# Folding the tokens twice over d in a spectral gate plus dense layer, with accumulating transfers and a new order

## The chip, the cores and the metric

One core of a Trainium2 chip. The metric is the device time of one execution in microseconds: the median of three runs of the kernel before is 382.09 (381.73 to 382.65). Lower is better.

## The reference, cut to what matters

```python
g = sigmoid((x * gate_w).sum(-1))            # x: 2048 tokens (s) by 512 (d), float32
X = rfft2(x, axes=(s, d)) * (w_r + 1j*w_i)   # 2048 by 257 weights
a = irfft2(X)
h = gelu(x @ w1 + b1)                        # 512 -> 1792
b = h @ w2 + b2                              # 1792 -> 512
out = g * a + (1 - g) * b
```

## The kernel before, in words

**Numbers in two parts.** [...] So each operand is split into a high part (a rounding copy on ScalarE) and a low part (source minus high, on VectorE), and a product is three matmuls: high by high, high by low, low by high. All go through the helper at L400.

**The spectral half.** The 2048 tokens are 16 groups `j` of 128. `forward(j)` does, for each group in the order `NORD` (0, 4, 8, 12, 1, 5, ...): load `xf`; form the sum and the difference `eo` of the two halves of d (L552, two half-width VectorE instructions); split it into `eoh` and `eol` (L557, L559); multiply by the cosine and sine table `cf` into `pd`, of 258 columns (257 frequencies and the column with the gate's weights); split `pd` into `xh`, `xl` (L589, L590); sum the gate's logit (L592); transform over 128 tokens by the table `tf` into `py`; combine into the group's plane `y` (L609 to L619). Since `eo` folds d once, 256 rows remain: two chunks `q` of 128, each with its own table half. After that come steps over the 16 planes on VectorE (`stage1`, `filt` with the weights `wf`, `stage4`), a small correction (`own_rows`: `own`, `pown`, `yfix`), and `inverse(c, h)`, eight times: turned planes `sw` (ScalarE), `pq`, the split `vh`, `vl` (L443, L444), products `pz` with `tg`, the split `zh`, `zl`, products `pa` with `ci`, a copy `od` (L850), and sums and differences `u`, `v`, `w` (L860 to L870).

**The dense half.** `mlp(half, c)` takes 512 tokens `c` and half of the 1792 hidden units: per 128 units a product `ph` (12 matmuls of 512 columns), gelu, a split into `g..h`, `g..l`; then four `po` of 21 matmuls each. The first half's `po` plus bias goes to a DRAM buffer `bacc` (L960, L965); the second half adds it: for `c` = 3 and 0 on VectorE (L963) and back into `bacc`, for 1 and 2 in `last` (L971, L973, L978) on the way out. `inverse` for 3 and 0 comes last of its `c` and itself subtracts the dense part times (1 - g) and writes `out` (L865, L873).

**The order.** Every piece is a `Step` with an engine, a planned cost and a rank. `Graph.schedule` plays the steps through with those costs; where an engine is free, the ready step with the lowest rank starts. What comes out is fixed: each engine then works through its own list in order and waits, by semaphores, where a datum isn't there. Ranks are a few constants (0 for `forward`, 1 `FEED`, 5 `BULK`). Buffers come from tagged pools (`slots`): `xr` has three, shared by the loads of `forward`, the token loads `xm` of the dense half, and `sw`. Transfers are issued by SyncE (SP); the kernel before issues none from GpSimd (POOL).

Of the kernel before, what the change touches and what calls it, by code (L numbers as in the profile page):

```python
# [26 lines left out]
CW = 272  # L27


FORD = np.concatenate([np.arange(0, HD, 2), np.arange(1, HD, 2), [HD]])  # L30
# [23 lines left out]
def _tables():  # L54

    d = np.arange(P)[:, None] + 0.5
    f = np.arange(NE)[None, :]
    th = 2 * np.pi * f * d / D
    cf = np.stack([np.cos(th), -np.sin(th)])
    cf[0][:, HD:] = 0.0  # L60
    cf[1][:, 0] = 0.0
    cf[1][:, HD + 1:] = 0.0
    cf = cf[:, :, FORD]

    cf = np.stack(_split(cf[:, :, :ND])).transpose(1, 2, 0, 3)
    cf = np.concatenate([cf, np.zeros((2, P, 2, CW - ND), np.float32)], 3)

# [48 lines left out]
SPARE = 0.4  # L116

# [215 lines left out]

@with_exitstack
def tile_kernel(ctx: ExitStack, tc: tile.TileContext, xt, w1, w2, b1, b2, x0g, wf, wrev, out, consts):
# [12 lines left out]
    slots = {"xr": 3, "wra": 3, "wrb": 2, "t2k": 7, "e2": 4, "z": 4, "ttab": 3, "xhl": 2, "wa": 2 * FA, "wb": 2 * FA, "hid": 2 * FA,  # L348
             "so": 2, "ba": 2, "bb": 1, "pf": 2, "pm": 4, "ti": 1}

    whole = ("xr", "wra", "wrb", "e2", "z", "ttab", "xhl", "wa", "wb", "hid", "so", "ba", "ctab", "gb")
# [59 lines left out]
    gs = one("gs", [P, 2, 2], parts=2)  # L411

    cft = buf("ctab", [P, 2, 2, 2, CW], F32R, "cf", parts=12)
    cfp = {(0, 0): (0,), (1, 0): (1,), (0, 1): (2, 3, 4), (1, 1): (5, 6, 7)}

    def cf(c, q):
        return cft.ap()[:, c, q]

    def cf_of(*cq):
        return [(cft, p) for k in cq for p in cfp[k]] + [(cft, g) for g in range(8, 12)]  # L420
# [5 lines left out]
    logit = one("logit", [P, NJ], parts=NJ, pool=sa)  # L426
# [20 lines left out]
    def minus(h, l, view, n, src, rest, rank):  # L447

        a(lambda: act.activation(view(l), view(h).bitcast(F32), AF.Copy, scale=-1.0), n, rest[0], rest[1], rank)
        acc(lambda: view(l), src, 256, [], rest[1], rank)  # L450


    def load_x(j, tag):
        x = buf("xr", [P, NQ, P], F32, f"x{tag}{j}")
        dma(lambda: sp.dma_start(x.ap(), xt[j]), 256, [], [x], j / 100 if tag == "f" and j in NORD[:4] else FEED)
        return x
# [17 lines left out]
    for j in NORD[1:4]:  # L474
        XF[j] = load_x(j, "f")
    for c in range(2):
        dma(lambda c=c: raw(cf(c, 0), cf_d[c]), 272, [], [(cft, k) for k in (c, 8 + c, 10 + c)], 0.6)
# [8 lines left out]
    gcol = [lambda k=k: cft.ap()[:, :, :, k, NE - 1] for k in range(2)]  # L486
    tiny(lambda: vec.tensor_copy(gcol[0](), gs.ap()), [gs], [(cft, 8), (cft, 9)])
    tiny(lambda: vec.tensor_tensor(gcol[1](), gs.ap(), gcol[0](), op=ALU.subtract), [gs, (cft, 8), (cft, 9)], [(cft, 10), (cft, 11)])
    for c in range(2):

        def same(c=c):
            s = slice(0, P) if c == 0 else slice(P, HD)
            vec.tensor_copy(cf(c, 1)[:, :, s], cf(c, 0)[:, :, s])

        def other(c=c):
            s = slice(P, HD) if c == 0 else slice(0, P)
            act.mul(cf(c, 1)[:, :, s], cf(c, 0)[:, :, s], -1.0)

        def end(c=c):
            vec.tensor_scalar(cf(c, 1)[:, :, HD:ND], cf(c, 0)[:, :, HD:ND], -1.0, None, op0=ALU.mult)  # L500

        for e, f, n, k in ((v, same, 256, 0), (a, other, 256, 1), (v, end, 2, 2)):
            e(f, n, [(cft, c)], [(cft, 2 + 3 * c + k)], 0)

    def load_small():
        dma(lambda: sp.dma_start(b1t.ap(), b1), 7, [], [b1t], 0.45)
        dma(lambda: sp.dma_start(b2t.ap(), b2), 2, [], [b2t])
        dma(lambda: sp.dma_start(rev.ap(), wrev), 32, [], [rev])
# [15 lines left out]
    def keep_x(c):  # L524

        late = [Y[NORD[9]]] if c == 0 else []
        for k, b in zip("hl", X[0, c]):
            for j in range(4):
                dma(lambda k=k, b=b, j=j: sp.dma_start(xs[c, k].ap()[:, :, j], b.ap()[:, :, j].bitcast(F32)), 256,
                    [(b, j), *late], [(xs[c, k], j)], 6)  # L530

    def load_mx(half, c):
# [4 lines left out]
        if half == 0:  # L537
            for j1 in range(4):
                split_1(X[0, c], load_x(c + 4 * j1, "m"), j1)
# [6 lines left out]
    def forward(j):  # L546
        first = j == 0
        x = XF.pop(j) if j in XF else load_x(j, "f")
        eo = buf("t2k", [P, 2, 2, P], F32, f"eo{j}", parts=2)
        h, l = (buf("e2", [P, 2, 2, P], F32R, f"eo{k}{j}", parts=2) for k in "hl")  # L550
        for s, op in ((0, ALU.add), (1, ALU.subtract)):
            v(lambda s=s, op=op: vec.tensor_tensor(eo.ap()[:, s], x.ap()[:, 0:2], x.ap()[:, 2:4], op=op), 256, [x],  # L552
              [(eo, s)], FEED)
        for k in (0, 1) if first else (slice(0, 2),):
            ps = [k] if first else [0, 1]
            sub = [[(b, p) for p in ps] for b in (eo, h, l)]
            a(lambda k=k: act.activation(h.ap()[:, k], eo.ap()[:, k], AF.Copy), 256 * len(ps), sub[0], sub[1],  # L557
              FEED)
            v(lambda k=k: vec.tensor_tensor(l.ap()[:, k], eo.ap()[:, k], h.ap()[:, k], op=ALU.subtract),  # L559
              256 * len(ps), sub[0] + sub[1], sub[2], FEED)  # L560
        if j % 4 == 0:
            if first:
                X[0, 0] = new_x(0, 0)
# [3 lines left out]
        ps = buf("pf", [P, 2, 512], F32, f"pd{j}", parts=2, pool=pq)  # L567

        def high(qs=(0, 1), cs=(0, 1)):
            for q in qs:  # L570
                for c in cs:
                    mm(ps.ap()[:, c, :NE], h.ap()[:, c, q], cf(c, q)[:, 0, :NE], q == 0, False)
                    mm(ps.ap()[:, c, :NE], h.ap()[:, c, q], cf(c, q)[:, 1, :NE], False, False)

        def low():
            for c in range(2):
                for q in range(2):
                    mm(ps.ap()[:, c, :NE], l.ap()[:, c, q], cf(c, q)[:, 0, :NE], False, q == 1)

        if first:  # L580
            for q in range(2):
                for c in range(2):
                    m(lambda q=q, c=c: high((q,), (c,)), NE, 2, [(h, c), *cf_of((c, q))], [(ps, c)], 0)
        else:
            m(high, NE, 8, [h, cft], [ps], 0)
        m(low, NE, 4, [l, cft], [ps], 0)
        xh = buf("z", [P, 2, 512], F32R, f"x{j}h")
        xl = buf("z", [P, 2, 512], F32R, f"x{j}l")
        a(lambda: act.activation(xh.ap()[:, :, :NE], ps.ap()[:, :, :NE], AF.Copy), 516, [ps], [xh], 0)  # L589
        v(lambda: vec.tensor_tensor(xl.ap()[:, :, :NE], ps.ap()[:, :, :NE], xh.ap()[:, :, :NE], op=ALU.subtract), 516, [ps, xh], [xl], 0)  # L590
        n = j % 4 * 4 + j // 4
        v(lambda: vec.tensor_reduce(logit.ap()[:, n:n + 1], ps.ap()[:, :, NE - 1], axis=mybir.AxisListType.X, op=ALU.add),  # L592
          30, [ps, xl], [(logit, n)], 0)
# [11 lines left out]
        for c in range(2):  # L605
            m(lambda c=c: s_high(c), NE, 2, [t, xh], [py[c]], 0)
# [477 lines left out]
```

## Time and profile before

| what | value |
|---|---|
| median of three runs | 382.09 us |
| the profiled execution: from its first to its last instruction (span) | 380.0 us |
| what the median has beyond that span | 2.1 us |
| PE busy | 374.5 us (99%) |
| VectorE (DVE) busy | 338.4 us (89%) |
| ScalarE (ACT) busy | 207.8 us (55%) |
| DMA, mean | 149 GB/s |

The page gives no other time of the profiled execution than its span, so all sums below are made against 380.0 us and 2.1 us are added at the end. PE's busy time is drawn with modelled ends; where PE's pace matters, the distance from one start to the next is the number to use. Lines "SPq" are transfers being issued.

### The profile page before, as it was taken

The numbers are of one execution on the slowest core, as the hardware profiler recorded it, in microseconds if no ns is written. First come the engines' busy times: TensorE is split into PE (matmuls) and PEld (weight loads), VectorE is DVE, ScalarE is ACT, GpSimd is POOL, SyncE is SP. The second block draws the span as 40 slices with busy tenths as digits, with TensorE's granted clock in tenths as the row PEclk, the third lists the DMA queues.
The fourth block names the chain that finished last, engine by engine and source line by source line (L and its number), as shares of the span: only waits on it lengthen the run. The fifth ranks groups of instructions, "written<-read, shape, count | busy, mean of one in ns | idle before, by whom it ended". The sixth has DMA issues, their size and how long they took to land.

```text
span 380.0 us, 5499 instructions
## 1 busy us (share of the span) xinstructions
PE 374.5 (99%) x1903; PEld 319.1 (84%) x1903; DVE 338.4 (89%) x705; ACT 207.8 (55%) x363; POOL 0.2 (0%) x4
## 2 busy tenths in 40 slices
PE   8999999999999999999999999999999999999996
PEld 7889999978888888888888888888888888888886
DVE  5999999879797999999999989976889889999962
ACT  6857678947622452265146594289315996525400
POOL 0000000000000000000000000000000000000000
PEclk9999999999999999999999999999999999999999
DMA  8976469895198014153342252314332055335031
GB/s 286 313 227 198 165 225 298 270 324 177 44 300 251 6 53 140 57 165 113 112 146 89 98 197 86 120 35 163 129 97 84 27 209 175 114 114 159 6 111 57
DMA packets 44307, 56.44 MB, mean 149 GB/s; under 512 B 4112, under 2 KB 27216, under 8 KB 43504
## 3 DMA queue, kind: packets, MB, share of 16 engines
q1 hardware_dynamic: 44136, 55.83, 45.1%
q8 instruction: 15, 0.25, 0.3%
q10 hardware_dynamic: 144, 0.26, 0.2%
q14 instruction: 12, 0.10, 0.1%
HBM read 39.16 MB, written 16.92 MB: 148 GB/s over the span
## 4 chain that ended last, share of the span: by engine, by line
PE 88%; ACT 5%; DMA 3%; DVE 2%; issue 1%; SPq 0%
PE ph L400 40%; PE po L400 34%; PE pd L400 5%; PE pz L400 3%; PE pa L400 3%; PE py L400 3%; DMA wf<-in_wf 2%; ACT sw L801 2%; DMA xf<-in_xt 1%; ACT sw L804 0%; ACT mxh L520 0%; ACT y L616 0%; ACT z10h L827 0%; DVE pq L808 0%; ACT pys L609 0%
## 5 line engine op out<-in xcount | busy, mean ns | idle before, releaser
L923 ACT ACTIVATE ph<-ph,b1t 128x512 f32<-128x512 f32 x56 | 37.1, 662 | 55.7 <-PE ph L400 55.2
L960 ACT ACTIVATE o<-po,b2t 128x512 f32<-128x512 f32 x16 | 11.1, 691 | 40.2 <-PE po L400 37.3
L801 ACT ACTIVATE sw<-y,al 64x512 f32<-64x512 f32 x32 | 23.2, 726 | 2.0 <-DVE y L664 1.4
L760 DVE TENSOR_TENSOR m<-y,wf 128x514 f32<-128x514 f32 x32 | 21.3, 691 | 0.0
L400 PE MATMUL pd<-cf,eoh 128*128 128x258 f32 x128 | 18.0, 283 | 0.0
L400 PEld LDWEIGHTS pd<-cf,eoh 128*128 128x128 f32 x128 | 16.8, 189 | 0.6 <-ACT eoh L557 0.2
L808 DVE SCALAR_TENSOR_TENSOR pq<-y,al,sw 128x256 f32<-128x256 f32 x32 | 14.2, 480 | 0.5 <-ACT sw L804 0.5
L552 DVE TENSOR_TENSOR eo<-xf 128x256 f32<-128x256 f32 x32 | 12.3, 420 | 0.0
L794 ACT ACTIVATE tg<-ti 128x128 fp32r<-128x128 f32 x16 | 4.9, 309 | 12.6 <-DVE ti L792 12.3
L559 DVE TENSOR_TENSOR eol<-eo,eoh 128x512 fp32r<-128x512 f32 (+1 forms) x17 | 11.0, 654 | 0.2
L616 ACT ACTIVATE y<-pys 64x257 f32<-64x257 f32 x24 | 10.1, 420 | 1.9 <-DVE pys L613 1.6
L557 ACT ACTIVATE eoh<-eo 128x512 fp32r<-128x512 f32 (+1 forms) x17 | 10.1, 603 | 1.1 <-DVE eo L552 1.1
L804 ACT ACTIVATE sw<-y 1x512 f32<-1x512 f32 x16 | 10.1, 632 | 0.4
L400 PE MATMUL pd<-cf,eol 128*128 128x258 f32 x64 | 10.1, 283 | 0.0
L978 DVE TENSOR_TENSOR o<-y,po 128x256 f32<-128x256 f32 x8 | 3.1, 419 | 7.6 <-PE po L400 7.6
L400 PEld LDWEIGHTS pd<-cf,eol 128*128 128x128 f32 x64 | 8.9, 190 | 0.3
L609 ACT ACTIVATE pys<-py 128x257 f32<-128x257 f32 x16 | 6.2, 386 | 5.0 <-PE py L400 4.6
L850 ACT ACTIVATE od<-pa 128x512 f32<-128x512 f32 x8 | 4.8, 594 | 7.2 <-PE pa L400 7.2
L521 DVE TENSOR_TENSOR mxl<-xm,mxh 128x512 fp32r<-128x512 f32 x12 | 7.9, 686 | 0.5 <-DMA xs0l<-mxl 0.3
L610 DVE TENSOR_TENSOR y<-py,pys 128x257 f32<-128x257 f32 x16 | 6.8, 426 | 1.5 <-ACT pys L609 0.9
L520 ACT ACTIVATE mxh<-xm 128x512 fp32r<-128x512 f32 x12 | 7.0, 626 | 1.3 <-DMA xm<-in_xt 1.3
L860 DVE TENSOR_TENSOR u<-pa,od 128x512 f32<-128x512 f32 x8 | 5.5, 688 | 1.9 <-ACT od L850 1.8
(673 smaller groups left out, 1297.4 us busy)
## 6 DMA issues: line engine op xcount, KB each, us to landing
bacc<-o SPq DMA_DIRECT2D x24, 256.0 KB, 3.5
wf<-in_wf SPq DMA_DIRECT2D x16, 257.0 KB, 3.2
tf<-tf SPq DMA_DIRECT2D x16, 256.0 KB, 3.4
bb<-bacc SPq DMA_DIRECT2D x16, 256.0 KB, 3.1
xf<-in_xt SPq DMA_DIRECT2D x15, 256.0 KB, 2.8
war<-in_w SPq DMA_DIRECT2D x14, 256.0 KB, 2.7
wbr<-in_w SPq DMA_DIRECT2D x14, 256.0 KB, 2.8
xm<-in_xt SPq DMA_DIRECT2D x12, 256.0 KB, 3.8
```

The costliest lines, as they stand in the source:

```text
L400: pe.matmul(ps, w, x, start=start, stop=stop)
L521: v(lambda: vec.tensor_tensor(l.ap()[:, :, j1], x.ap()[:, :NQ], h.ap()[:, :, j1], op=ALU.subtract), 512, [x, (h, j1)], [(l, j1)], rank)
L552: v(lambda s=s, op=op: vec.tensor_tensor(eo.ap()[:, s], x.ap()[:, 0:2], x.ap()[:, 2:4], op=op), 256, [x], [(eo, s)], FEED)
L557: a(lambda k=k: act.activation(h.ap()[:, k], eo.ap()[:, k], AF.Copy), 256 * len(ps), sub[0], sub[1], FEED)
L559: v(lambda k=k: vec.tensor_tensor(l.ap()[:, k], eo.ap()[:, k], h.ap()[:, k], op=ALU.subtract), 256 * len(ps), sub[0] + sub[1], sub[2], FEED)
L616: a(lambda o=o, i=i: act.activation(Y[j].ap()[o:o + HP, 1], pys.ap()[i:i + HP, 1], AF.Copy), 257, [(pys, 1)], [(Y[j], 1 + k)], 0, more=0.1)
L760: v(lambda mk=mk, k=k, y=y, w=w: vec.tensor_tensor(mk.ap(), y.ap(), w.ap()[:, k:k + 1, :ND].to_broadcast([P, 2, ND]), op=ALU.mult), 514, [ ...
L801: a(lambda sw=sw, y=y, o=o, i=i: act.activation(sw.ap()[o:o + HP], y.ap()[i:i + HP, ::-1, :HD], AF.Copy, scale=al.ap()[i:i + HP, 0:1]), 51 ...
L804: a(lambda sw=sw, y=y, j=j: act.activation(sw.ap()[HP:HP + 1], y.ap()[HP:HP + 1, ::-1, :HD], AF.Copy, scale=math.cos(math.pi * j / NJ)), 5 ...
L808: v(lambda sw=sw, pq_=pq_, y=y, j=j, k=k, op=op: vec.scalar_tensor_tensor(pq_.ap()[:, k], y.ap()[:, k, :HD], al.ap()[:, 1 + j:2 + j], sw.a ...
L923: a(lambda f=f, ps=ps: act.activation(ps.ap(), ps.ap(), AF.Gelu_apprx_tanh, bias=b1t.ap()[:, f:f + 1]), 600, [b1t], [ps], 0.9 if half else ...
L960: a(lambda o=o, ps=ps, q=q: act.activation(o.ap(), ps.ap(), AF.Identity, bias=b2t.ap()[:, q:q + 1]), 600, [b2t, ps], [o])
```

## The change

1. **A second fold.** Of `eo`, the sums and differences of its two chunks are formed too (`cl`, L686), so odd and even frequencies each need 128 rows only. The table `cf` holds, per cosine or sine and per parity, high and low parts side by side: 130 + 130 columns. The high tokens are multiplied by all 260 columns in one matmul, the low ones by the first 130. `pd` then holds the two parts beside each other, and the split adds them: per group one copy and two half-width VectorE instructions for each of `c` = 0, 1 (L717 to L719) instead of one of each over 516. The logit is copied by ScalarE (L720) and summed once at the end.
2. **Folds by transfer.** For the last ten groups of `NORD` the first fold isn't computed on VectorE: SP loads `eo`, ScalarE negates half of it (L666), and an accumulating transfer from POOL adds the other half.
3. **Second-half weights.** Their low parts come from a negated copy on ScalarE and an accumulating transfer of the weights (14 in all) instead of 14 VectorE subtractions.
4. **Dense sums.** For `c` = 3, 0, 1 the second half's `po` is negated by ScalarE and added into `bacc` by an accumulating transfer; `combine` multiplies by (1 - g), and either this or the spectral part is added into `out` by another (for `c` = 1 the dense part is written first and `y` added). For `c` = 2 the dense part is added into `y` by transfers. `last` keeps one subtraction for `c` = 2 only.
5. **Narrow low products** in `inverse`: `vl` times the first 128 columns of `tg` only, where it was 256. Sums `uv`, `y` are formed in wide instructions (L982, L985).
6. **Buffers and order.** `xm` gets four slots of its own. `inverse` runs in the order 3, 0, 2, 1 (before 1, 2, 3, 0), the one for 1 after `mlp(1, 1)`. All ranks are replaced by a table of one number per step.

```diff
+LATE_X = 1
+FOLD_DMA = 6
+INV = (3, 0, 2, 1)
+SUM_FIRST = (1,)
...
+RANKS = (
+    10, -264, 217, 4, 0, 151, 201, 939, 1419, 551, 744, 809, 819, 1847, 2273, 396, 835, 1120, 930, 1330, 1567, 407, 491,
...
     def forward(j):
-        for s, op in ((0, ALU.add), (1, ALU.subtract)):
-            v(lambda s=s, op=op: vec.tensor_tensor(eo.ap()[:, s], x.ap()[:, 0:2], x.ap()[:, 2:4], op=op), 256, [x],
-              [(eo, s)], FEED)
...
+        by_dma = NORD.index(j) >= FOLD_DMA
+        if by_dma:
+            eo = buf("xr", [P, 2, 2, P], F32, f"eo{j}")
+            dma(lambda: sp.dma_start(eo.ap().rearrange("p a b c -> p (a b) c"), xt[j]), 256, [], [eo])
+            a(lambda: act.activation(eo.ap()[:, 1], eo.ap()[:, 1], AF.Copy, scale=-1.0), 256, [], [eo], FEED)
+            acc(lambda: eo.ap(), lambda: xt[j].rearrange("p (a b) c -> p a b c", b=2)[:, ::-1], 256, [], [eo], FEED)
...
+        for k, op in enumerate((ALU.add, ALU.subtract)):
+            v(lambda k=k, op=op: vec.tensor_tensor(quarter(cl, k), eo.ap()[:, :, 0], eo.ap()[:, :, 1], op=op), 256, [eo],
+              [(cl, k)] if j % 4 == 0 or by_dma else [cl], FEED)
...
-                    mm(ps.ap()[:, c, :NE], h.ap()[:, c, q], cf(c, q)[:, 0, :NE], q == 0, False)
-                    mm(ps.ap()[:, c, :NE], h.ap()[:, c, q], cf(c, q)[:, 1, :NE], False, False)
...
+        def prod(c, x, n, start):
+            for k in range(2):
+                mm(pd[c].ap()[:, k, :n], x.ap()[:, c, k * P:(k + 1) * P], cf(c, k, n), start, not start)
...
+            m(lambda c=c: prod(c, h, 2 * NC, True), 2 * NC, 2, [h, *cf_of(c)], [pd[c]], 0)
+            m(lambda c=c: prod(c, l, NC, False), 240, 2, [l, *cf_of(c)], [pd[c]], 0)
...
+            a(lambda c=c: act.activation(two(xh, c), body(c, 0), AF.Copy), 258, [pd[c]], [(xh, c)], 0)
+            v(lambda c=c: vec.tensor_tensor(two(xl, c), body(c, 0), two(xh, c), op=ALU.subtract), 258, [pd[c], (xh, c)], [(xl, c)], 0)
+            v(lambda c=c: vec.tensor_tensor(two(xl, c), two(xl, c), body(c, 1), op=ALU.add), 258, [pd[c]], [(xl, c)], 0)
...
     def inverse(c, h):
+                    n = 2 * P if x is vh else P
+                    mm(ps.ap()[:, ft, k, :n], x.ap()[:, k, ft * P:(ft + 1) * P], t.ap().rearrange("p a b -> p (a b)")[:, :n], first, not first)
...
+            if c in SUM_FIRST:
+                acc(lambda k=k: part(c, h, k), lambda w=w: w.ap()[:, :, :2 * P], 256, [w], [(OUT[c], 2 * h + k)], 4)
...
     def load_w(n, f):
+        minus(h, l, lambda b: b.ap(), 512, (w1 if n == "a" else w2)[f], ([h], [l]), 3)
...
     def mlp(half, c):
+            elif c != 2:
+                a(lambda o=o, ps=ps: act.activation(o.ap(), ps.ap(), AF.Copy, scale=-1.0), 512, [ps], [o], 2)
+                acc(lambda q=q: bacc[c].ap()[:, q].rearrange("p a b -> p (a b)"), lambda o=o: o.ap(), 256, [o],
+                    [(bacc[c], 2 * q), (bacc[c], 2 * q + 1)], 4)
```

The helper of the accumulating transfers stood in the kernel before, unused: `acc(...)` issues `nc.gpsimd.dma_start(dst, src, accum_op=ALU.add)`.

Three places show what the new order moves. The first is TensorE's list where the first group of tokens enters. Names carry a running number behind the last underscore; `ph0_2` is the product for tokens `c` = 0, hidden block 2, `pd4` that of group 4, `pd01` that of group 0, sine. Before:

```order
L400 MATMUL ph0_2_226<-mxh00_111,wa2l_172 128x512
L400 MATMUL pd0_261<-cf_121,eoh0_221 128x258 x8
L400 MATMUL pd4_278<-cf_121,eoh4_257 128x258 x8
L400 MATMUL pd0_261<-cf_121,eol0_241 128x258 x4
L400 MATMUL pd4_278<-cf_121,eol4_272 128x258 x4
L400 MATMUL ph0_3_314<-mxh00_111,wa3h_250 128x512
```

The same place in the kernel after the change:

```order
L517 MATMUL po0_000_302<-g0_1h_252,wb1h_228 128x512
L517 MATMUL po0_000_302<-g0_1l_261,wb1h_228 128x512
L517 MATMUL po0_000_302<-g0_1h_252,wb1l_286 128x512
L517 MATMUL pd00_384<-cf_198,eoh0_258 128x260 x2
L517 MATMUL pd00_384<-cf_198,eol0_290 128x130 x2
L517 MATMUL pd01_395<-cf_198,eoh0_258 128x260 x2
L517 MATMUL pd01_395<-cf_198,eol0_290 128x130 x2
L517 MATMUL ph0_6_404<-mxh00_109,wa6h_338 128x512
```

Twelve `pd` matmuls of a group became eight, four of them half as wide, and group 0 now enters behind `ph0_5` and two thirds of a `po` step instead of behind `ph0_2`.

The second place is the end of TensorE's list, at the last `pa` of the last `inverse` (`pa01` is that of `c` = 0, `h` = 1). Before, with `po1_210` begin the last 84 matmuls: 21 each of `po1_210` and `po1_220`, and 42 of half width:

```order
L400 MATMUL pa01_3988<-z01l_3964,ci_1134 128x256 x2
L400 MATMUL pa01_3988<-z01h_3956,ci_1134 128x256 x4
L400 MATMUL pa01_3988<-z01l_3964,ci_1134 128x256 x2
L400 MATMUL po1_210_4019<-g2_7h_3809,wb7h_2278 128x512
L400 MATMUL po1_210_4019<-g2_7l_3813,wb7h_2278 128x512
```

After:

```order
L517 MATMUL po1_220_4042<-g2_13h_3976,wb13l_2498 128x512
L517 MATMUL pa11_4086<-z11l_4059,ci_1479 128x256 x2
L517 MATMUL pa11_4086<-z11h_4039,ci_1479 128x256 x4
L517 MATMUL pa11_4086<-z11l_4059,ci_1479 128x256 x2
L517 MATMUL po1_230_4111<-g2_7h_3659,wb7h_2293 128x256
L517 MATMUL po1_230_4111<-g2_7l_3669,wb7h_2293 128x256
```

Behind the last `pa` only the 42 matmuls of 256 columns of `po1_230` and `po1_23256` are left.

The third place is the end of POOL's list, which before held no transfer at all (`bacc1` is the dense sum of `c` = 1, `bb2q` the dense part of `c` = 2, `y` as source the spectral part of `c` = 1):

```order
L508 DMA bacc1_1291<-o1_12_3798 128x512
L508 DMA bacc1_1291<-o1_13_3803 128x512
L508 DMA y_484<-bb20_2071 128x256
L508 DMA y_484<-bb21_2125 128x256 x2
L508 DMA out_0<-y_484 128x2x256 x2
L508 DMA y_484<-bb23_3817 128x256 x2
L508 DMA out_0<-y_484 128x2x256 x2
```

The last two pairs are new waits in a row: the sums for `c` = 2 stand behind the first half of the spectral part of `c` = 1, and the very last transfers are its second half.

300 lines of the change are left out of this document (151 added, 149 removed), and 108 rows, old and new, of the table RANKS.

## The prediction

> **What bounds the kernel now.** I read the page's busy times and slices first, then the chain of waits, then the windows. The page:
>
> ```profile
> span 380.0 us, 5499 instructions
> PE 374.5 (99%) x1903; PEld 319.1 (84%) x1903; DVE 338.4 (89%) x705; ACT 207.8 (55%) x363; POOL 0.2 (0%) x4
> PE   8999999999999999999999999999999999999996
> DVE  5999999879797999999999989976889889999962
> PEclk9999999999999999999999999999999999999999
> ```
>
> TensorE (PE) is busy in every slice at the full granted clock; VectorE (DVE) is close behind. In the chain of waits, in order of time (start, length, what), nearly all is PE:
>
> ```profile
> 47.27 2.88 PE pd L400 x24
> 80.75 0.70 DVE mxl L521
> 81.50 10.95 PE ph L400 x47
> 119.93 19.04 PE ph L400 x84
> 352.68 0.95 PE pz L400 x8
> 362.22 14.59 PE po L400 x84
> 376.83 0.42 DVE o L978
> ```
>
> These rows give the pace of matmuls back to back, start to start: 19.04/84 = 0.227 us at 512 columns, 2.88/24 = 0.120 at 258, 0.95/8 = 0.119 at 256. The one VectorE piece in the middle is a real hole: PE waited 0.7 us for `mxl`. At the end 3.2 us follow PE's last matmul. By windows (length, then busy time of each engine):
>
> ```profile
> 6.18:70.00 63.82, 63.80 (x414) 58.12 (x415) 60.51 (x146) 49.38 (x100) 0.00 (x0) 1.00 0.76 250
> 215.00:376.83 161.83, 161.57 (x834) 137.99 (x832) 139.78 (x284) 86.73 (x145) 0.00 (x0) 1.00 0.34 115
> 376.83:380.00 3.17, 0.00 (x0) 0.00 (x0) 0.42 (x1) 0.00 (x0) 0.00 (x0) 1.00 0.12 41
> ```
>
> So from 6.18 to 376.83 us PE is the bound, with DVE at 95% (60.51 of 63.82) in the forward stage. What shortens PE's list shortens the time, unless DVE or a transfer then comes late.
>
> **1. PE's list.** Before, `pd` has 16 x 12 = 192 matmuls of 258 columns: 192 x 0.120 = 23.0 us. After, 64 have 260 columns (64 x 0.121 = 7.7 us) and 64 have 130. In `pz` 64 of 128 fall from 256 columns (64 x 0.119 = 7.6 us) to 128. All else on PE keeps its count. With y for a narrow matmul the saving is 23.0 - 7.7 + 7.6 - 128 y = 22.9 - 128 y. No row shows a narrow one with a new weight load. From the 256- and 512-column rows the slope is 0.108/256 = 0.42 ns a column, so y would be 0.119 - 0.054 = 0.065 if columns alone counted. As the other end I take the widest row, 0.227. What speaks for a value between is the weight load:
>
> ```profile
> 374.83 0.28 PE L400 MATMUL po<-g_9h,wb9h 128*128 128x256 f32 x1
> 374.84 0.19 PEld L400 LDWEIGHTS po<-g_9l,wb9h 128*128 128x128 f32 x1
> 374.95 0.28 PE L400 MATMUL po<-g_9l,wb9h 128*128 128x256 f32 x1
> ```
>
> The load of the next weights begins when the matmul before begins (374.84 after 374.83), and its own matmul begins 0.11 us after the load (374.95). If this 0.11 is the load's own length, a narrow matmul can't follow faster. I take y = 0.113, nearest to these rows: saving 22.9 - 14.5 = **8.4 us** (14.6 at 0.065, a loss of 6.2 at 0.227).
>
> On this the Trainium skill has two rules. "TensorE: Matmul & The Clock Gate", section "LDWEIGHTS (loading the stationary operand)", lets a load take its columns over 1.2 GHz, 107 ns for 128; by that the saving would be 9.2 us, and the 0.11 us above agrees. The same page, "Back-to-back issue gap", gives 81 ns a matmul for a stream of load and matmul pairs at 128 columns; by that it would be 12.5 us, but the 131 ns that it gives at 512 columns don't agree with the 227 ns here.
>
> **2. The hole at 80.75.** `mxl` stood on DVE behind a `filt` step that waited for its weights. In the new order the four splits for `c` = 1 stand among the forward steps, ahead of all `filt` steps, with loads from slots of their own: **-0.7 us** (0 if another wait takes its place).
>
> **3. The first 35 us on DVE.** The second fold and the two-part split add DVE work just where it is scarce. The rows for its prices:
>
> ```profile
> 48.26 1.09 DVE L552 TENSOR_TENSOR eo<-xf 128x256 f32<-128x256 f32 x3
> 4.63 0.23 DVE L484 TENSOR_TENSOR gs<-xf 128x2 f32<-128x2 f32 x2 [3.63 <-DMA xf<-in_x0g]
> 362.89 0.69 DVE L860 TENSOR_TENSOR u<-pa,od 128x512 f32<-128x512 f32 x1 [0.16 <-ACT od L850]
> 363.50 0.68 DVE L861 TENSOR_TENSOR v<-pa,od 128x512 f32<-128x512 f32 x1
> ```
>
> Start to start a wide instruction takes 0.61 (362.89 to 363.50), I count 0.62; a half-width one 1.09/3 = 0.36, I count 0.35; a small one 0.23/2, I count 0.12. DVE gets its first datum at 4.6. In the new order, up to the end of group 4's split `x4l`, DVE has 27 wide, 30 half and 10 small: 16.7 + 10.5 + 1.2 = 28.4, so it ends at 33.0 at the earliest. PE, starting at 6.18 as now, has before the matmul that needs this 24 of 256, 87 of 512, 8 wide and 8 narrow `pd`, 8 `py`: 2.9 + 19.7 + 1.0 + 0.9 + 1.0 = 25.5, so it is there at 31.7. It waits about **+1.3 us** (0 with DVE 5% faster; 3.2 with a wide piece at the full 0.69 of its row). The same count before, at its tightest place (`eol12`: 26 wide, 21 half, 12 small, 24.9 + 4.6 = 29.5; PE 23.2 + 6.2 = 29.4), comes out even, and there PE indeed runs on. Later in the forward stage there is more room after the change than before: the ten last groups lose two half-width folds each, and the `ph` and `po` of `c` = 1 now stand between the groups, so that PE reaches `py15` at some 105 us of its list where DVE needs 92 + 4.6.
>
> **4. DVE, ACT and POOL later.** By the two lists DVE goes from 394 wide and 233 half to 361 and 257: -33 x 0.62 + 24 x 0.35 = -12 us, 326 of some 373 (87%). ACT gains the 14 negated weights, 12 negated `po`, 10 half-width negations, 32 logit copies and the halved `xh`: about +29 us, 237 or 63%. Both lie beside PE's matmuls and I cost them at nothing; without that cover a wide piece late costs PE its 0.62 us. POOL gains 56 accumulating transfers: 10 folds, 14 weights, 12 `po`, 12 into `out`, 8 into `y`. What one costs isn't in the trace. Plain transfers of 256 KB (size, time to landing):
>
> ```profile
> xs1l<-mxl SPq DMA_DIRECT2D x4, 256.0 KB, 5.2
> xs2h<-mxh SPq DMA_DIRECT2D x4, 256.0 KB, 2.6
> xf<-in_xt SPq DMA_DIRECT2D x15, 256.0 KB, 2.8
> ```
>
> It can't land earlier than the fastest, 2.6; two of the slowest one behind the other, for a second pass over the data, give 10.4. I take A = 6.0: the slowest, and 0.8 for 256 KB more at the 323 GB/s or so that the busiest slices show:
>
> ```profile
> GB/s 286 313 227 198 165 225 298 270 324 177 44 300 251 6 53 140 57 165 113 112 146 89 98 197 86 120 35 163 129 97 84 27 209 175 114 114 159 6 111 57
> ```
>
> *Folds.* A fold holds one of three `xr` buffers from its load to its second fold: 2.8 + about 1 on ACT + 6.4 (issue and landing) + 0.7 on DVE with some waiting, 12 us. By its list and the paces above PE wants the ten groups 4.9 us apart (57 to 101 us), so a buffer may take 14.6. Hidden. *Weights* are wanted 30 us after they can start. Hidden. *The dense sum of `c` = 1* goes from PE's last `po1_120` through ACT and POOL into `bacc1`, back by SP, and DVE's next-but-few instruction waits for it in order; behind it stand the last gelu splits and `z10l`, which PE's last `pa` need. By list times the chain fits with A up to about 6.4: hidden, barely.
>
> **5. The end.** Before, the last `inverse` ended 14.6 us before PE did; now 42 x 0.119 = 5.0 us. After its last matmul come `od` on ACT (0.6 and 0.05 to start), four wide DVE pieces (2.5): 3.2 us, then the issue of two transfers (0.4) and A. The other way out is 5.0 + 0.4 + 2.8 (380.0 less 377.25) + 0.3 = 8.5 us as before. 3.6 + 6.0 = 9.6: **+1.1 us** (0 at A up to 4.9, +5.5 at 10.4).
>
> **Sum.** 380.0 - 8.4 - 0.7 + 1.3 + 1.1 = 373.3; with the 2.1 us around the span, **375.4 us**. A measurement can tell a difference of about 0.2%, 0.8 us, from none.
>
> **Rivals.**
>
> *a) Narrow matmuls follow by their columns.* If the load's 0.11 us hides behind an earlier matmul, y = 0.065 and 6.1 us more go: 369.3. For it: PE's loads already run one matmul ahead. Against: never closer than 0.11 in the rows. Chance 0.08. The 81 ns of the Trainium skill's page, weighed in 1, would lie between this case and the forecast, at 371.3.
>
> *b) The order closes PE's small holes.* Start to start PE's list before adds up to 1311 x 0.2267 + 290 x 0.119 + 290 x 0.120 = 366.5 us without the warm-up matmuls, and 376.8 - 6.2 = 370.6 pass; 0.7 of the 4.1 is the hole of term 2, the rest are short holes between groups. If the new order closes 3 us of them: 372.4. Chance 0.06.
>
> *c) DVE is late more often.* Each late split in the forward stage, and the chain in 4, stops PE as in 3. With three more such stops of 1.5 us: 380. For it: DVE at 95% and in order. Against: the list counts above. Chance 0.13; this ends on either side of no change.
>
> *d) Accumulating transfers land late; slower than before.* At A = 10 the fold ring needs 16 us for a buffer where PE gives 14.6: 10/3 x 1.4 = 4.7 us late in the forward stage; the `bacc1` chain is 3.6 late, and the end 4.0 more: 375.4 + 12.3 = 387.7. It decides from A of about 9, where the end takes 3.0, the chain 2.6 and the ring 1.3, together the 6.7 that the forecast gains. For it: POOL issues nothing today, so nothing shows; DVE is busy nearly all the time. Against: the DMA engines are busy 34% of the window from 215 us (its last share but one), so bandwidth isn't short. Chance 0.05. The Trainium skill, "SBUF — State Buffer", section "SBUF: two separate sides", says that POOL can't write a transfer's descriptors while DVE holds their shared port in certain modes; that would raise A in just this way, and no run here shows it yet.
>
> *e) The narrow matmuls save nothing.* At y = 0.227, the 512-column pace, the first term turns into +6.2: 390.0. It decides from y = 0.165. Against: from 512 to 256 columns the time falls to 0.52 of what it was, with no sign of a floor. Chance 0.02.
>
> **How the numbers follow.** The forecast, 375.4, has 0.66; its own range is 372.5 to 378.5. The range for 8 in 10 is 370.8 to 380.5: out fall a) (0.08), d) and e) (0.07) and a third of c) (0.04). Faster by over 0.2% (below 381.3): 0.66 + 0.08 + 0.06 + 0.08 of c) = 0.88. Within 0.2%: 0.03 of c). Slower: 0.02 of c), d) and e) = 0.09.
>
> **What would show it.** Term 1: eight `pd` of a group in 0.94 us instead of twelve in 1.44; narrow ones 0.11 start to start. Term 2: no wait of PE for `mxl`. Term 3: PE waits between 25 and 35 us for `x0l` or `x4l`. Term 4: DVE near 326 us, no wait of DVE for `ba` or of ACT and DVE for folded `eo`; POOL's time to landing near 6. Term 5: the chain ends in a transfer of `y`, 4 to 5 us after PE's last matmul. The forecast is wrong if PE shows holes after 110 us, or landings above 9.

## The result, and the profile after the change

The changed kernel takes **401.69 us** (median of four, 400.82 to 402.97) against 382.06 us (381.73 to 382.65) for the kernel before on the same chip: a ratio of 1.051, 95% interval 1.0485 to 1.0539. It is 5% slower where 375.4 us was forecast. In the tables below a median is over all executions of a kernel, while a ratio leaves out those that lie over 1.5% above the kernel's fastest; the changed kernels with more scratch memory spread over 2%, so there the two can disagree.

The page of the profile after, busy times and slices:

```profile
span 400.4 us, 5572 instructions
PE 376.6 (94%) x1839; PEld 314.6 (79%) x1839; DVE 326.6 (82%) x682; ACT 226.5 (57%) x444; POOL 57.1 (14%) x60
PE   7999999969999999999999999999999769999990
PEclk9999999979999999999999999999999969999997
```

VectorE's 326.6 us are the 326 of the forecast. But PE now has holes near 85 us and near 315 to 330 us and a long end, and its granted clock falls at the first two. The waits of PE (us in all, how often, the longest):

```profile
PE py L517 <- DVE x6l L719: 3.2, 1, 3.2
PE pz L517 <- ACT v2h L560: 2.3, 1, 2.3
PE po L517 <- DVE g_11l L561: 2.3, 1, 2.3
PE ph L517 <- ACT mxh L633: 1.9, 1, 1.9
...
PE po L517 <- DVE g_13l L561: 1.0, 1, 1.0
PE pd L517 <- DVE x14l L719: 0.8, 1, 0.8
```

No wait for `mxl` is left, but VectorE and ScalarE come late elsewhere. What VectorE waited for between 50 and 112 us, and from issue to landing the accumulating transfers (size, median us):

```profile
DVE cl L686 <- DMA eo<-in_xt: 10.9, 4, 4.3
...
bacc<-o POOLq DMA_DIRECT2D x12, 256.0 KB, 5.5
eo<-in_xt POOLq DMA_DIRECT2D x10, 256.0 KB, 5.3
out<-ba POOLq DMA_DIRECT2D x8, 256.0 KB, 4.5
y<-bb POOLq DMA_DIRECT2D x8, 128.0 KB, 3.8
out<-y POOLq DMA_DIRECT2D x4, 256.0 KB, 4.3
```

The landings are where the forecast had them (6.0), or faster. The folds are late all the same. POOL's timeline shows why (start, length of the issue, and in brackets how long POOL waited ahead of it):

```profile
67.71 1.21 POOL L508 DMA_DIRECT2D eo<-in_xt  x1 [6.39 <-ACT logit L720]
74.18 1.22 POOL L508 DMA_DIRECT2D eo<-in_xt  x1 [5.25 <-ACT ph L1063]
79.03 1.21 POOL L508 DMA_DIRECT2D eo<-in_xt  x1 [3.63 <-DVE g_3l L561]
84.59 1.22 POOL L508 DMA_DIRECT2D eo<-in_xt  x1 [4.35 <-issue]
```

The page puts these waits down to whatever ended last, but none of the named engines is what POOL needs. ScalarE's negations, which POOL does need, came earlier, and the chain has when one of these transfers landed:

```profile
71.75 0.42 ACT L666 ACTIVATE eo<-eo 128x256 f32<-128x256 f32 x1
72.12 0.41 ACT L666 ACTIVATE eo<-eo 128x256 f32<-128x256 f32 x1
81.04 0.41 ACT L666 ACTIVATE eo<-eo 128x256 f32<-128x256 f32 x1
...
79.03 5.24 DMA eo<-in_xt
```

The fold negated at 72.12 is issued at 79.03; the next, negated at 81.04, at 84.59, 0.3 us after the one before it landed (79.03 + 5.24 = 84.27). From 53.45 us on POOL issues a fold every 5.95 us on average (seven steps to 95.07), and PE wants them 4.9 us apart; six of the seven issues begin 0.32 us after the fold before has landed, and the seventh (90.48) waits for its own negation. The same at the end:

```profile
379.54 1.23 POOL L508 DMA_DIRECT2D out<-y  x1 [15.47 <-DVE y L985]
384.01 1.22 POOL L508 DMA_DIRECT2D out<-y  x1 [3.24 <-DVE o L1114]
...
389.98 1.21 POOL L508 DMA_DIRECT2D out<-y  x1 [0.44 <-DVE y L985]
394.62 1.23 POOL L508 DMA_DIRECT2D out<-y  x1 [3.43 <-issue]
```

Each pair of sums into `out` is issued 4.5 to 4.6 us apart, one landing, while smaller transfers follow each other at once. A fold or a sum into `out` is 256 rows of 1 KB; a transfer into `bacc`, a weight or a half `y` is 128 rows. That gave the first theory, **R**: POOL builds a transfer's rows in a scratch memory (1024 bytes, `dynamic_dma_scratch_size`, unchanged by the change), which by these waits holds 256 + 128 rows but not 512, and POOL stands still until room is free. Its rivals: **Q**, the in-order queues of ACT, SP and POOL and the landing itself set the pace; **O**, the new table of ranks is at fault.

**Where the 20 us lie.** From the distance between the starts of each matmul of PE and the next I subtracted the price of the matmul (0.227, 0.120, 0.119 us, 0.121 for 260 columns and 0.113 for a narrow one). What is left, summed by stretch, is time lost on PE's list; the last column is the time from PE's last start to the end of the span. The rows with an x are kernels of the experiments below.

| us lost | 0 to 40 | 40 to 110 | 110 to 290 | 290 to 340 | from 340 | after PE's last start |
|---|---|---|---|---|---|---|
| before | 3.5 | 1.3 | 0.6 | 0.4 | 0.1 | 3.5 |
| after | 5.4 | 10.2 | 2.9 | 9.3 | 1.1 | 9.3 |
| x scratch1536 | 3.7 | 2.9 | 3.7 | 2.0 | 0.3 | 6.2 |
| x long_rows | 3.4 | 5.4 | 3.0 | 7.7 | 0.7 | 8.8 |
| x folds_vec | 3.2 | 4.2 | 5.3 | 7.9 | 0.9 | 9.1 |
| x tail_vec | 3.0 | 2.6 | 3.7 | 0.5 | 0.4 | 4.2 |

PE's list is 8.4 us shorter; 23.0 us more are lost on it and 5.8 after it: together the 20.4 us between the two spans.

**The clock makes the holes dearer.** After the hole at 83 us, PE at 89 us (starts of 512-column matmuls):

```profile
89.67 0.63 PE L517 MATMUL ph<-mxl,wa6h 128*128 128x512 f32 x1
90.10 0.63 PE L517 MATMUL ph<-mxh,wa6l 128*128 128x512 f32 x1
90.52 0.63 PE L517 MATMUL ph<-mxh,wa6h 128*128 128x512 f32 x1
...
91.59 0.39 PE L517 MATMUL ph<-mxh,wa6h 128*128 128x512 f32 x1
91.82 0.39 PE L517 MATMUL ph<-mxl,wa6h 128*128 128x512 f32 x1
```

0.43 us apart instead of 0.23, half the rate. From 86.71 to 91.35 pass 4.6 us for 2.4 us of list; after the holes at 321 to 325 us, 5.5 us for 2.7 (324.85 to 330.35): 5.0 of the 20 us are the clock's answer to holes. The Trainium skill, "TensorE: Matmul & The Clock Gate", "Part 1: The HAM clock gate", says that PE falls to half its clock after an idle window of some 3.4 us and needs as long a busy one to come back. Half rate agrees; as for the length, see the last section.

### The profile page after: what moved, and what is told of

Same layout as the page of the kernel before. It is cut to its first block, busy times and chain, and to the rows that moved or that the text cites. A ratio compares the mean times of both kernels' runs of the same rounds, so it can differ in the third digit from the quotient of the medians.

```text
span 400.4 us, 5572 instructions
## 1 busy us (share of the span) xinstructions
PE 376.6 (94%) x1839; PEld 314.6 (79%) x1839; DVE 326.6 (82%) x682; ACT 226.5 (57%) x444; POOL 57.1 (14%) x60
## 4 chain that ended last, share of the span: by engine, by line
PE 57%; DMA 15%; DVE 11%; ACT 9%; issue 5%; POOL 1%; SPq 1%; POOLq 0%; ACTq 0%; DVEq 0%
PE ph L517 28%; PE po L517 21%; DMA ti<-ti 5%; DMA eo<-in_xt 4%; DMA bacc<-o 3%; ACT sw L929 3%; PE pz L517 2%; PE pd L517 2%; PE py L517 2%; DMA xr<-in_xt 2%; DMA wf<-in_wf 2%; PE pa L517 1%; ACT ph L1063 1%; ACT sw L932 1%; DVE m L888 1%
## 5 line engine op out<-in xcount | busy, mean ns | idle before, releaser
L508 POOL DMA_DIRECT2D eo<-in_xt x10 | 12.3, 1234 | 83.5 <-DVE x0l L719 29.0
L888 DVE TENSOR_TENSOR m<-y,wf 128x514 f32<-128x514 f32 x32 | 20.4, 687 | 0.0
L686 DVE TENSOR_TENSOR cl<-eo 128x256 f32<-128x256 f32 x28 | 11.4, 418 | 10.9 <-DMA eo<-in_xt 10.9
L508 POOL DMA_DIRECT2D out<-ba x8 | 9.7, 1214 | 64.4 <-DMA out<-y 26.4
L508 POOL DMA_DIRECT2D bacc<-o x12 | 11.7, 1034 | 37.8 <-ACT o L1102 31.4
L517 PE MATMUL pd<-cf,eoh 128*128 128x260 f32 x64 | 13.8, 299 | 1.2 <-DVE x14l L719 0.8
L982 DVE TENSOR_TENSOR uv<-pa,od 128x512 f32<-128x512 f32 x16 | 10.3, 682 | 2.3 <-ACT od L979 2.3
L517 PE MATMUL pd<-cf,eol 128*128 128x130 f32 x64 | 11.1, 256 | 0.0
L985 DVE TENSOR_TENSOR y<-uv 128x512 f32<-128x512 f32 x16 | 10.6, 686 | 0.1
L688 ACT ACTIVATE eoh<-cl 128x512 fp32r<-128x512 f32 x14 | 8.9, 634 | 2.8 <-DVE cl L686 2.8
L508 POOL DMA_DIRECT2D y<-bb x8 | 7.6, 1047 | 19.0 <-DVE y L985 15.6
```

What stands on the lines that cost most here:

```text
L508: return add("pool", 2 * kb / 340, 3.6, lambda: nc.gpsimd.dma_start(dst(), src(), accum_op=ALU.add), reads, writes, rank)
L517: pe.matmul(ps, w, x, start=start, stop=stop)
L686: v(lambda k=k, op=op: vec.tensor_tensor(quarter(cl, k), eo.ap()[:, :, 0], eo.ap()[:, :, 1], op=op), 256, [eo], [(cl, k)] if j % 4 == 0 or ...
L688: a(lambda: act.activation(h.ap(), cl.ap(), AF.Copy), 512, [cl], [h], FEED)
L888: v(lambda mk=mk, k=k, y=y, w=w: vec.tensor_tensor(mk.ap(), y.ap(), w.ap()[:, k:k + 1, :ND].to_broadcast([P, 2, ND]), op=ALU.mult), 514, [ ...
L982: v(lambda i=i, op=op: vec.tensor_tensor(uv.ap()[:, i], ps.ap()[:, 0], od.ap(), op=op), 512, [ps, od], [(uv, i)], 2)
```

## The experiments

Lines of code are those of the changed kernel; times are against the kernel before on the same chip.

**1. More scratch memory (scratch1536).**

```diff
-            w = buf("ttab", [P, 2, 288], F32, f"wf{k2}")
+            w = buf("ttab", [P, 2, 264], F32, f"wf{k2}")
...
-    nc = bacc.Bacc("TRN2", target_bir_lowering=False, num_devices=1, dynamic_dma_scratch_size=1024)
+    nc = bacc.Bacc("TRN2", target_bir_lowering=False, num_devices=1, dynamic_dma_scratch_size=1536)
```

> Edit: the scratch memory in which POOL builds its transfers grows from 1024 to 1536 bytes (the tile of wf shrinks from 288 to 264 columns to make room, its used columns stay); each engine's list is word for word that of the changed kernel. Theory R (room): POOL cannot issue while more rows are open than the scratch holds. In the profile after, a transfer of 256 rows is issued only when the one before has landed (79.03 + 5.24 = 84.27, next issue 84.59), while two of 128 rows go out back to back; so 1024 bytes hold 384 rows and not 512, and 1536 should hold two of 256. Then folds go out as soon as ACT has negated them, the 3.2 us hole of PE at 83 us and its low clock go, the bacc sums of 295 to 300 us go out 3 us earlier, and the last two transfers of out follow each other at once: 383 to 391 us, about 387. Theory Q (queues): POOL waits for ACT and SP, which are in order, and the size of the scratch changes nothing: 400 to 403 us.

Measured: 382.87 us (ten executions, 381.06 to 390.86), before 381.72; ratio 1.0038 (1.0007 to 1.0068). With every engine's list unchanged (both traces show the same order), 18.8 of the 20 us are gone, a little more than R expected. Its page and POOL's issues:

```profile
span 380.8 us, 5572 instructions
PEclk9999999999999999999999999999999999999999
...
69.89 2.47 POOL L508 DMA_DIRECT2D eo<-in_xt  x2 [3.59 <-ACT eo L666]
...
373.03 2.48 POOL L508 DMA_DIRECT2D out<-y  x2 [4.42 <-DVE y L985]
```

Two folds, and the two last sums, now go out back to back (2.47 us for two), POOL's wait is for the negation that it needs, and the clock stays up. Theory Q falls.

**2. Half the rows (long_rows).** The same fold, from a second copy of the tokens with the halves swapped, which the kernel gets as an input; scratch memory as in the change.

```diff
-            acc(lambda: eo.ap(), lambda: xt[j].rearrange("p (a b) c -> p a b c", b=2)[:, ::-1], 256, [], [eo], FEED)
+            acc(lambda: eo.ap().rearrange("p a b c -> p (a b c)"), lambda: xs2[j].rearrange("p a c -> p (a c)"), 256, [], [eo], FEED)
```

> Edit: the ten folds by transfer read a second copy of the tokens in which the two halves of d are swapped, so that each fold is 128 rows of 2 KB and not 256 of 1 KB; bytes, number of transfers, scratch memory and every list stay. Theory R: three folds of 128 rows fit at a time, so POOL waits for no landing up to 100 us, the forward stage gains 5 to 8 us; the sums into out and the tail stay as they are: 394 to 397 us. Theory Q: the landing of an accumulating transfer, 5 to 6 us whatever its rows, and the queues set the pace: 399 to 403 us.

Measured: 392.94 us, ratio 1.0289 (1.0235 to 1.0343): 9 us gained, slightly more than expected. POOL's issues in the same stretch:

```profile
72.73 1.75 POOL L508 DMA_DIRECT2D eo<-in_xs  x2 [3.86 <-ACT logit L720]
82.47 0.88 POOL L508 DMA_DIRECT2D eo<-in_xs  x1 [7.99 <-ACT eo L666]
85.66 0.87 POOL L508 DMA_DIRECT2D eo<-in_xs  x1 [2.31 <-ACT eo L666]
87.82 0.86 POOL L508 DMA_DIRECT2D eo<-in_xs  x1 [1.29 <-DVE x10l L719]
```

The same bytes in 128 rows aren't held up, with 1024 bytes: it is the rows that count, not the transfer or its landing. In the table the loss moves where R put it: 40 to 110 us falls from 10.2 to 5.4, while 290 to 340 us and the end, where `out` still goes in 256 rows, change little (7.7 and 8.8, from 9.3 each).

**3. Folds on VectorE (folds_vec)**: `FOLD_DMA = 16`.

> Edit: all sixteen folds on VectorE (FOLD_DMA = 16); the ranks of the three steps of each fold stay with the three steps that take their place. Theory R: POOL is idle up to 150 us, VectorE has 20 half-width instructions more (7 us) in a stage in which it was busy for about 42 of 60 us, so PE's holes between 50 and 110 us go for the most part: 392 to 396 us. Theory O (the order itself is bad, the folds are not): the holes stay, VectorE gets later still: 400 to 406 us.

Measured: 393.86 us, ratio 1.0311 (1.0280 to 1.0341), as R said. About as good as shorter rows: the folds by transfer cost some 8 us at 1024 bytes, the later sums the other 10 or so. This split is rough: without the transfers the planner also puts about 160 of PE's 1839 matmuls in other places.

**4. Without the table (plain_ranks)**: the three lines that set `s.rank` are left out.

> Edit: the table of ranks is left out, so that the steps are ordered by the few constants in the code, all else as after the change. Theory O: the table's order is what costs the 20 us: below 390 us. Theory R: POOL's waits belong to the transfers and not to the table; they stay: 396 to 410 us.

Measured: 406.91 us, ratio 1.0649 (1.0591 to 1.0707). O falls: the table is worth 5 us even here.

**5. The end by VectorE (tail_vec)**, on top of 1536 bytes.

```diff
-            if c in SUM_FIRST:
-                acc(lambda k=k: part(c, h, k), lambda w=w: w.ap()[:, :, :2 * P], 256, [w], [(OUT[c], 2 * h + k)], 4)
+            if (c, h) == (1, 1):
+                v(lambda w=w, b=b: vec.tensor_tensor(w.ap()[:, :, :2 * P], w.ap()[:, :, :2 * P], b.ap(), op=ALU.add), 512, [b], [w])
+                dma(lambda w=w, k=k: sp.dma_start(part(c, h, k), w.ap()[:, :, :2 * P]), 256, [w], [(OUT[c], 2 * h + k)], 4)
+            elif c in SUM_FIRST:
```

> Edit, on top of the 1536 bytes: for the last half of c = 1 the dense part stays in its ba tile, VectorE adds it to y (two wide instructions) and SP writes out plainly, where before the dense part was written first and y added by the last two accumulating transfers. With 1536 bytes PE's last matmul starts at 374.65 and the span ends at 380.8, 6.2 us later; in the kernel before it was 3.5 us. Theory T (the two last accumulating transfers set the end): DVE is done at about 374.5, a plain transfer issued and landed by 377.7, so the last o of c = 2 sets the end again, at 378.3: 380.0 to 381.0 us. Rival U: the end follows PE and o anyway, or the two instructions make VectorE late: 382.5 to 384 us.

Measured: 381.85 us (twelve, 378.06 to 385.96), ratio 0.9971 (0.9940 to 1.0002). The median lies between the ranges of T and U, so the times leave them undecided; the length of the end speaks for T. The profiled execution spans 376.6 us, its PE starts the last matmul 4.2 us before the end (6.2 with the transfers), and the chain ends in `o`:

```profile
367.62 5.03 PE po L518 x42
372.65 0.02 issue
372.67 0.42 DVE o L1124
```

That alone wouldn't tell T from U, as the chain of scratch1536 ends in `o` too. There the last sum of POOL lands at 379.44 us and the last `out<-o` at 379.61, 3.8 us after its issue; here it lands 2.2 us after it.

**6. Wide low products (wide_low)**, on top of 1536 bytes: the low products over the whole table.

> Edit, on top of the 1536 bytes: the low products in pd and pz run over both halves of their table, 260 and 256 columns where they had 130 and 128 (what is added is low times low); every list keeps its length. Against scratch1536 on the same chip. By starts in the traces a narrow matmul costs y = 0.097 us, so 64 x 0.024 + 64 x 0.022 = 2.9 us more, 385.2 to 386.4. If a narrow one cost its columns alone (0.065, rival a), 7.0 us more, 389 to 391; at the 0.113 of the forecast 0.9 us more, 383.3 to 384.2; if PE's list weren't the bound, 382.4 to 383.4.

Measured: 383.24 us (380.01 to 389.25), ratio 1.0004 (0.9976 to 1.0031), against 382.87 for scratch1536. The 2.9 us that I expected from the starts aren't there, nor the 7.0 of rival a. The median lies just under the range for y = 0.113 and inside the one for a list of PE that isn't the bound, so the times decide no more than that. The traces do: all lists are those of scratch1536, so the starts can be compared place by place. From a narrow matmul to the fourth behind it (distances over 0.3 us left out) the wide products take 0.7 us more in `pd` and 0.4 in `pz`, 64 of each: y = 0.110 and 0.112.

**7. Both remedies (long_1536, both_1536).** 1536 bytes and 128 rows; then the end by VectorE with them.

> Edit: 1536 bytes and the folds with 128 rows of 2 KB from the swapped copy. Theory R: two transfers of 256 rows fit already, POOL's waits for room in the forward stage are nearly gone (issues at 69.89 and 71.1 follow each other at once), so little is left to win: 381.5 to 383 us. Rival: the stage is still bound by room or by the time that POOL takes for an issue (1.22 us for 256 rows, 0.86 for 128): 378 to 380.5 us.

> Edit: 1536 bytes, folds with 128 rows of 2 KB, and the last half of c = 1 added by VectorE. The gains of the two add up if they lie in different stages: by theories R and T 379.3 to 380.8 us, just under the kernel before (381.7). By U and the rival of the fold rows: 378 to 382.5 us, with the tail still 6 us long in the profile.

Measured: 383.97 us, ratio 1.0031 (1.0000 to 1.0062), and 382.06 us, ratio 0.9950 (0.9923 to 0.9978). Shorter rows on top of the room bring nothing, as R said, though the median is 1 us above R's range. both_1536 misses the 379.3 to 380.8 us of R and T together, though its end is as short as that of tail_vec (4.3 us). Its twelve executions range from 377.91 to 387.14 us, where 35 of the kernel before lie within 380.95 and 383.50. Its ratio says half a per cent faster, its median not; I wouldn't call it a better kernel. Its own profile, at 380.9 us, shows one source of the spread:

```profile
53.33 0.33 PE L518 MATMUL py<-x5l,tf 128*128 128x258 f32 x1
55.46 0.50 PE L518 MATMUL ph<-mxh,wa0h 128*128 128x512 f32 x1 [1.80 <-ACT pys L738]
55.80 0.39 PE L518 MATMUL ph<-mxl,wa0h 128*128 128x512 f32 x1
...
57.21 0.63 PE L518 MATMUL ph<-mxh,wa0h 128*128 128x512 f32 x1
57.63 0.63 PE L518 MATMUL ph<-mxl,wa0h 128*128 128x512 f32 x1
...
60.14 0.39 PE L518 MATMUL ph<-mxl,wa1h 128*128 128x512 f32 x1
```

A hole of 1.8 us, with one of 0.4 us at 52.8 us ahead of it, is followed by half clock from 56.5 to 60 us. In the profiles of tail_vec and long_1536 the hole at this place is 0.3 to 0.4 us and the clock stays up. So an execution in which PE has to wait here pays twice; what made the wait longer in this execution, and whether this is the whole spread, no run shows.

**8. Narrow products alone (before_narrow)**: part 5's narrow `pz` in the kernel before.

> Edit: the kernel before, with one part of the change alone: in inverse the low products run over the first 128 columns of the table only (what is left out is low times low); no list changes its length or order. PE is the bound there, so 64 matmuls shorter by 0.119 - y should show one to one. At y = 0.097 as the starts in the changed kernel's trace give: 1.4 us less, 380.3 against 381.7. At 0.065 (columns alone) 3.5 us less, 378.2. At 0.113 (the forecast) 0.4 us less, 381.3. And where the 512-column pace of this trace is 0.227, as in the kernel before, and not 0.230, as in all the kernels after the change, the slower pace belongs to the change and not to the chip.

Measured: 381.53 us (eleven, 380.76 to 382.20), before 381.71; ratio 0.9990 (0.9979 to 1.0001), or 0.4 us less: **y = 0.113**, the forecast's, with an interval of 0.107 to 0.120, which leaves out the 0.097 that the starts suggest and the 0.065 of rival a. Compared place by place with the trace of before, as in 6, the narrow products save 0.5 us: y = 0.111. The trace shows where the difference goes:

```profile
260.23 0.33 PE L400 MATMUL pz<-tg,v2l 128*128 128x128 f32 x2
260.40 0.45 PE L400 MATMUL pz<-tg,v2h 128*128 128x256 f32 x2
260.69 0.34 PE L400 MATMUL pz<-tg,v2l 128*128 128x128 f32 x2
260.87 0.44 PE L400 MATMUL po<-g_7h,wb7h 128*128 128x512 f32 x1
261.15 0.39 PE L400 MATMUL po<-g_7l,wb7h 128*128 128x512 f32 x1
```

A pair of narrow ones takes 0.17 to 0.18 us instead of 0.24, but the next pair of wide ones 0.29 instead of 0.24, and the 512-column one after the last 0.28 instead of 0.23. Most of what a narrow matmul saves, its neighbour gives back. The weight loads show why: in this stretch they begin 0.108 to 0.120 us apart (260.24, 260.35, 260.46, 260.58, 260.69, 260.80), and in the whole trace no two begin less than 0.108 us apart. In this trace the 512-column pace is that of the kernel before.

**9. The slower pace (before_pool, aligned).** The mean distance between the starts of two 512-column matmuls (holes left out) is 0.2277 us in the kernel before and in before_narrow, and 0.2300 to 0.2302 in the profile after and in experiments 1 to 5: over 1311 of them 3 us, and most of what is lost between 110 and 290 us. Two guesses: that a POOL which is awake slows PE (the last sum of the kernel before issued by POOL), and the place of PE's operands in memory.

> Edit: the kernel before, with the very last of the transfers that inverse writes out issued by POOL, plainly, in place of SP; POOL so waits from the start to 350 us. In all kernels after the change a 512-column matmul takes 0.230 us start to start, in the kernel before 0.227; over 1311 of them 3 to 4 us. Theory W (POOL awake and waiting is what slows PE's pace): 384.5 to 386 us and 0.230 in the trace. Rival: POOL waiting costs PE nothing: 381.5 to 382.2 us and 0.227.

> Edit: the changed kernel with 1408 bytes of scratch memory, wf of 272 columns and an unused tile of 64 bytes, so that every operand of PE starts at a multiple of 128 bytes, as in the kernel before; in the changed kernel they start at 64 past one. Theory R: 1408 bytes hold 528 rows or more, two transfers of 256, so the time is that of scratch1536, 382 to 384 us. Theory L (the place of the operands sets PE's pace): 0.227 us for 512 columns and 3 to 4 us less, 378.5 to 380 us. If 1408 bytes hold only one transfer of 256 rows, 398 to 402 us.

Measured: before_pool 381.89 us, ratio 1.0007 (0.9997 to 1.0017), pace 0.2277; aligned 383.63 us, ratio 1.0021 (0.9993 to 1.0050), pace 0.2296. Neither. `aligned` also gives a second point for R: with 1408 bytes two transfers of 256 rows already go out together (the last two `out<-y` in 2.46 us).

**10. Folds on VectorE with room (folds_vec_tail).**

> Edit: tail_vec (1536 bytes, the last half of c = 1 added by VectorE) with all sixteen folds on VectorE. Theory R: with room in the scratch the folds by transfer are hidden or nearly so, and VectorE's 7 us more in the forward stage cost PE something: 382 to 385 us, against 381.9 for tail_vec. Theory O: the folds by transfer are a loss also with room, as each goes through SP, ACT, POOL and VectorE in their orders: 378 to 381 us.

Measured: 383.59 us, ratio 1.0052 (1.0033 to 1.0071). Against tail_vec it is 1.7 us slower, as R said, with the spreads overlapping: with room the folds by transfer are at least no loss. As in folds_vec, the edit also moves some 160 of PE's matmuls, so the 1.7 us are not the folds' alone.

**11. Weights by transfer alone (before_weights)**: part 3 in before_narrow.

> Edit: before_narrow and part 3 of the change with it, nothing else: the low parts of the second half's weights by a negated copy and an accumulating transfer of 128 rows each (14 in all) in the kernel before, with its 1024 bytes; in inverse low times low is left out. Theory R: up to three transfers of 128 rows fit, so none of them waits for room; VectorE is relieved of 14 wide instructions that were hidden: the time is that of before_narrow, 381 to 382 us. If accumulating transfers as such were the loss, whatever the room: 384 us or more, with holes of PE behind them. For the pace: if accumulating transfers on POOL's queue make a 512-column matmul 0.230 us, the trace shows it from 150 us on and the time rises by 2 to 3 us; if not, 0.227 all along.

Measured: 383.95 us, ratio 1.0057 (1.0039 to 1.0075), 2.4 us above before_narrow, where I expected nothing; the rival, accumulating transfers as a loss in themselves, had 384 or more, with holes. The pace stays at 0.2277, so accumulating transfers don't make it either. The loss is in new holes of PE, of which these are the largest:

```profile
PE po L400 <- DVE o L970: 1.2, 1, 1.2
...
PE pz L400 <- DVE z21l L831: 0.7, 1, 0.7
```

Both stand behind VectorE and far from the transfers (237 and 270 us; POOL's last issue but one is at 206.88). The edit did more than its text says: the planner ordered what follows in another way. PE's list is that of before_narrow up to 214.7 us; behind it some 330 of its matmuls stand in other places. So the run doesn't separate the transfers from the order; that it is the order, is argued from the place of the holes.

## Why the prediction was wrong, point by point

- **Term 4 failed, and with it the whole.** The step is "so a buffer may take 14.6. Hidden.", and in the same way "hidden, barely" for the dense sums: each of POOL's 56 transfers was priced by its landing A. A was right (5.3 us for a fold, 6.0 forecast), but I let any number of transfers be on their way at once. With 1024 bytes POOL holds one of 256 rows. So the folds come every 5.95 us where PE wants them 4.9 us apart; `bacc` sums wait behind sums into `out` (294.82, then 300.31 us), behind them SP's load of `ba`, behind that in SP's order the load of `ti`, for which VectorE waits 6.4 us, and PE 2.3 us for `g_11l` behind it. scratch1536 shows the size: 18.8 us between two medians, some 5 of them the clock's.
- **Term 1 was right**, in its mechanism too: y is 0.110 to 0.113 (before_narrow, wide_low), and the weight loads set that floor. Only the sign that it named, narrow matmuls 0.11 us from start to start, isn't what one sees: inside a pair they start 0.06 us apart, and the matmul behind them pays. The 8.4 us are real and were given back elsewhere.
- **Term 2 was right**: no wait for `mxl`.
- **Term 3 was wrong.** PE doesn't wait between 25 and 35 us. The count for VectorE was good: in scratch1536 `x4l` ends at 33.4 us, where 33.0 was forecast. But PE's matmul at that place needs only the first half of `x4l`, which is there at 31.6, and PE starts it at 32.8. Instead PE waits 1.9 us at 7 us for `mxh`, whose load landed late; with the same lists in scratch1536 this wait is 0.3 us, and POOL's first transfer goes out only at 29.49, so it is the spread of the plain transfers.
- **Term 5 was mis-sized**: +1.1 forecast, +5.8 measured, +2.7 with room. I priced the issue at 0.4 us for two transfers; POOL takes 1.2 us for each of 256 rows, and with 1024 bytes the second starts one landing later.
- **Term 4's other sums**: VectorE 326.6 (forecast 326), ScalarE 226.5 (237).
- **What scratch1536 still has above the forecast**, 380.8 against 373.3: 6.6 us more than before lost on PE's list, where terms 2 and 3 made it 0.6, and 2.7 instead of 1.1 at the end, together the 7.5 within 0.1. Some 3 of the 6.6 are the pace, most of the rest short waits for VectorE (`z01l`, `g_5l`, `g_4l`, `g_1l`, `x6l`, 3.1 us). "PE shows holes after 110 us" was the right alarm. So rival b went the other way: the new order opens small holes where the old one had closed them. And of its 4.1 us in the kernel before some 1.3 were no holes: over the whole list a 512-column matmul takes 0.2277 us, and b) reckoned with 0.2267.
- **Rivals.** a) and e) fall by y = 0.11. c) happened, four times and more, but VectorE was late because it waited itself (10.9 us for folds). d) had the sign, the three places and nearly the kind: folds, `bacc` and the end. Its lever was wrong: it needed A above 9, and its condition never came (the longest took 8.5 us). The Trainium skill's rule that it leaned on ("SBUF — State Buffer", "SBUF: two separate sides") would have shown as late landings beside a busy VectorE; with VectorE 82% busy the medians are 3.8 to 5.5 us, so nothing here speaks for it. I gave d) 0.05 because I looked for the price of a transfer, never for how many the issuer can have open; the trace of before, in which POOL issues none, couldn't show it, which was a reason for a wider bound and not for "hidden".

## What to carry to other kernels

Where a change brings in a queue that the profile has not shown, bound not only how long one transfer takes but how many can be open, and in what unit (here rows, by the scratch memory). A wait whose named releaser has nothing to do with the waiting instruction, and which ends when the transfer before it lands, looks like a wait for room; one edit of that room, with every list unchanged, tests it. And price a shorter instruction by the time of what follows it too, best in a kernel whose executions agree.

## What the runs showed of the hardware

- POOL's issue: 1.2 us for 256 rows of 1 KB, 0.86 to 0.92 for 128 rows of 1 or 2 KB, where it doesn't follow another at once; open at once at 1024 bytes: 384 rows, not 512; at 1408 and 1536: 512.
- No two weight loads begin less than 0.107 us apart in any trace here, and a 128-column matmul with a new load costs 0.11 us on the average, where one of 256 columns costs 0.119.
- A hole of PE of 1.8 us with one of 0.4 us ahead of it (both_1536) was followed by half the clock, for about 3.5 us and beginning 1 us after PE had started again; one of 2.3 us (311 us in the profile after) went by without it. The 3.4 us of idling that the Trainium skill's page names weren't needed, and the length of one hole alone doesn't decide.
- PE's 512-column pace is 1% slower in every kernel after the change, in stretches in which it does the same work as before. The table of ranks (plain_ranks, 0.230), the alignment of the operands to 128 bytes (aligned), an awake POOL (before_pool) and 14 accumulating transfers (before_weights) aren't it; the cause stays open.
